# Gated linear attention and an MLP in one kernel: step 1 without halves, one transfer queue, a planner that may let an engine wait, attention visits placed anew

## The chip, the cores and the metric

The kernel runs on one core of one Trainium2 chip. Its engines are TensorE (PE in the rows; PEld is its loading of weights, which runs beside the products), VectorE (DVE), ScalarE (ACT), GpSimd (POOL) and SyncE (SP), which here only issues DMA transfers. The metric is the device time of one execution in microseconds (us); the median of several runs counts.

## The reference

Attention with a decaying state, and behind it a two-layer MLP on its output:

```python
f = 1 / (1 + exp(-f_logit))                  # q, k, v, f: (4 batches, 8 heads, 768 tokens, 48)
for t in range(768):
    state = f[:, :, t, :, None] * state + einsum('bhd,bhe->bhde', k[:, :, t], v[:, :, t])
    y[:, :, t] = einsum('bhd,bhde->bhe', q[:, :, t], state)
x = y.transpose(0, 2, 1, 3).reshape(3072, 384)
h = x @ w_in                                  # 384 -> 2048
g = where(h >= 1, h, where(h <= -1, 0, (h + 1)**2 / 4))
out = g @ w_out                               # 2048 -> 384
```

All is in float32.

## The kernel before

**Steps and units.** The 768 tokens are cut into six steps (0 to 5) of 128 tokens in each of the four batches, so that a step has 512 columns. A step's attention gives `x`, three tiles of 128 rows by 512 columns. The hidden layer is done in 16 pieces of 128 rows; one piece of one step is a *unit*, 96 in all, 0 to 95: units 0 to 15 belong to step 0, 16 to 31 to step 1, and so on. A unit has two halves on TensorE. The first half (`unit_1`, L250) puts nine products into one of two PSUM banks `ph`, the second half (`unit_2`, L274) puts nine products into the three banks `po`, which gather one step's output. Nine and not three, because each float32 operand is split into a high and a low part and three of the four combinations are summed: `w_hi` and `w_lo` for the weights, `ghi` and `glo` for the activation; `x` holds both parts. Between the halves stand five instructions: `act` (L253, ScalarE), `act` (L256, ScalarE), `act` (L261, VectorE), the rounding to `ghi` (L264, ScalarE) and the rest `glo` (L267, VectorE). The first half of unit u+1 lies between the two halves of unit u.

**Attention.** The eight heads are four pairs, and a step's attention runs two pairs at a time: gates (sigmoid L483, two scans L485 and L492, products with k and q L494 and L496), transposed keys `kn`, scores (L675), outputs (L762 from the states, L730 from the step's own values) and new states (L823; the first step uses L802 and others). The results leave PSUM as a rounded high part (ScalarE, L713) and a low part (VectorE, L714) into `x` and, for the fourth pair, into `y`. Those rows are then carried to where `x` wants them by six on-chip DMA transfers, the *moves* x<-y (L292); similar moves kq<-kq bring gated keys and queries into place. A first half of the next step's first unit needs all of its step's moves.

**Halves.** Step 1 alone (`HALVES = 1`) is handled in two halves of 256 columns: its gates, its attention and its moves come once for each two batches, and its first six units (`FIRST = 6`) are run in pairs on one half of the columns and then on the other, so that these units can start when only half of `x` is there. `order_of` holds that order.

**Weights.** They arrive packed in 25 pieces `raw`; ScalarE (L378, L383) and VectorE (L380, L384) unpack each into `w_hi` and `w_lo` during the first steps. Later the remaining transfers `raw` bring the packed weights once more, and VectorE reduces them (L394) for a test at the end: if some weight does not fit the packed form, a fallback computes everything again. `test` makes one number of it with a product of one column (L976) and a comparison; all engines load that number, `flag`, behind their last instruction (L1055) and branch on it (L1056).

**Who sets the order.** The code does not issue instructions where it stands. Each call of `add` gives a class `Plan` an operation with its engine, a cost and what it depends on; `order` then runs through time with those costs, and at each engine picks the operation that is most urgent (`late`, worked out from the end backwards) among those that could start. TensorE's operations keep the order of the code; for the others the planner's order is final, and each engine executes its own in that order. Where the plan shows a long gap on TensorE, `warm` fills it with products of zeros (L328). Where attention work stands among the units comes from two tables: `TURNS` (at which unit a pair's keys are transposed) and `VISITS` (at which units its scores, its states and its outputs come). A transfer is issued by `dma` (L287, SyncE) or `move` (L292), which takes SyncE and ScalarE in turn:

```python
def move(k, dst, src, *deps, near=NEAR):
    e, q = (("SP", nc.sync), ("ACT", nc.scalar))[k % 2]
```

An engine that issues a transfer waits at that point until what the transfer reads and overwrites is free, and whatever stands behind it on that engine waits with it.

## Time and profile before

| | before |
|---|---|
| runs | 480.68, 481.96, 482.08 us; median 481.96 us |
| span of the profiled execution | 480.9 us |
| TensorE busy | 470.6 us, 98% of the span |
| VectorE busy | 369.3 us, 77% |
| ScalarE busy | 264.7 us, 55% |
| GpSimd busy | 31.0 us, 6% |
| bytes read and written | 44.63 and 4.72 MB, 103 GB/s over the span |

The profile is of one execution. Times in it count from the start of the span. Matmuls are pipelined: the next starts before the one ahead is over, so the pace of TensorE is read from start to start and not from a row's duration. "PEld" rows are weight loads; a wait that ends there shows up on the products only if it outlasts the products ahead. In brackets a row tells how long its engine was idle before it and what released it. "SPq" and "ACTq" are the issues of transfers.

### The profile page before, as it was taken

To read this page: it belongs to the slowest core of one execution; us is meant where nothing else is said; L and a number is where in the kernel's file an instruction comes from. 1 tells how busy PE (TensorE), PEld (TensorE's weight loads), DVE (VectorE), ACT (ScalarE), POOL (GpSimd) and SP (SyncE) were. 2 spreads that over 40 slices of the span, in tenths; PEclk is the share of its full clock that TensorE was granted. 3 is DMA by queue.
4 is the path that set the end of the run, shared out by engine and by line. 5 is a ranking of instruction groups with operands and counts; after the bars stand their busy time and mean duration, and the time that the engine had idled before them with its cause. 6 is when DMAs were issued, how large, how long until landed. Compare 5 with 4: busy or idle time off the path is not lost.

```text
span 480.9 us, 11259 instructions
## 1 busy us (share of the span) xinstructions
PE 470.6 (98%) x4661; PEld 383.3 (80%) x4661; DVE 369.3 (77%) x715; ACT 264.7 (55%) x486; POOL 31.0 (6%) x76
## 2 busy tenths in 40 slices
PE   9989999999999999999999999999999999999994
PEld 4877888889988887887878878887888888888883
DVE  7979998859989999999997899675657545653332
ACT  4489998846355364555545464464545444544451
POOL 4201220100010101001000001000000000000000
PEclk9999999999999999999999999999999999999998
DMA  8689758055023061124144142143410242510001
GB/s 300 199 283 325 231 158 240 6 209 182 1 78 121 4 176 67 35 90 156 57 117 142 58 165 67 45 130 103 153 45 6 85 121 87 154 44 0 3 0 72
DMA packets 21866, 54.29 MB, mean 113 GB/s; under 512 B 3472, under 2 KB 6672, under 8 KB 21808
## 3 DMA queue, kind: packets, MB, share of 16 engines
q1 hardware_dynamic: 20464, 51.43, 33.1%
q10 hardware_dynamic: 1344, 2.07, 1.9%
q8 instruction: 38, 0.62, 0.6%
q14 instruction: 20, 0.16, 0.1%
HBM read 44.63 MB, written 4.72 MB: 103 GB/s over the span
## 4 chain that ended last, share of the span: by engine, by line
PE 73%; DVE 17%; DMA 5%; issue 2%; ACT 1%; SPq 0%; ACTq 0%; DVEq 0%
PE po L274 34%; PE ph L250 32%; DVE kn L708 6%; DMA raw<-in_w 2%; DVE glo L267 2%; PE pa L730 2%; PE pa L762 2%; DVE act L261 1%; DVE w L485 1%; DMA kq<-in_kq 1%; DVE kq L494 1%; PE ph L675 1%; DVE am L681 1%; DVE kq L496 1%; DMA f<-in_f 1%
## 5 line engine op out<-in xcount | busy, mean ns | idle before, releaser
L250 PE MATMUL ph<-x,w_hi 128*128 128x512 f32 (+1 forms) x606 | 146.8, 378 | 0.2
L250 PEld LDWEIGHTS ph<-x,w_hi 128*128 128x128 f32 x606 | 109.3, 188 | 22.5 <-DVE am L681 1.8
L253 ACT ACTIVATE act<-ph,half 128x512 f32<-128x512 f32 x96 | 65.8, 686 | 100.8 <-PE ph L250 91.6
L261 DVE SCALAR_TENSOR_TENSOR act<-ph,act 128x512 f32<-128x512 f32 x96 | 66.0, 687 | 62.2 <-ACT act L256 61.0
L264 ACT CAST ghi<-act 128x512 fp32r<-128x512 f32 x96 | 59.5, 620 | 85.5 <-DVE act L261 80.9
L274 PE MATMUL po<-ghi,w_hi 128*128 128x512 f32 (+1 forms) x306 | 87.6, 391 | 1.4 <-ACT ghi L264 1.3
L274 PE MATMUL po<-ghi,w_lo 128*128 128x512 f32 (+1 forms) x306 | 83.5, 378 | 0.0
L274 PE MATMUL po<-glo,w_hi 128*128 128x512 f32 (+1 forms) x306 | 83.4, 378 | 0.0
L267 DVE TENSOR_TENSOR glo<-act,ghi 128x512 fp32r<-128x512 f32 x96 | 66.0, 687 | 20.3 <-ACT ghi L264 18.2
L250 PE MATMUL ph<-x,w_lo 128*128 128x512 f32 (+1 forms) x303 | 81.2, 376 | 0.0
L708 DVE STREAM_TRANSPOSE kn<-kq 32x128 f32<-32x128 f32 x224 | 67.7, 302 | 3.5
L274 PEld LDWEIGHTS po<-glo,w_hi 128*128 128x128 f32 x306 | 55.3, 188 | 11.5 <-DVE glo L267 0.7
L274 PEld LDWEIGHTS po<-ghi,w_lo 128*128 128x128 f32 x306 | 55.4, 188 | 11.1
L274 PEld LDWEIGHTS po<-ghi,w_hi 128*128 128x128 f32 x306 | 52.6, 188 | 14.0 <-ACT ghi L264 4.3
L250 PEld LDWEIGHTS ph<-x,w_lo 128*128 128x128 f32 x303 | 55.3, 188 | 10.5
L256 ACT ACTIVATE act<-act 128x512 f32<-128x512 f32 x96 | 60.7, 632 | 3.0
L394 DVE TENSOR_REDUCE ok<-raw 128x1 f32<-128x512 f32 x48 | 31.5, 679 | 5.2 <-DMA raw<-in_w 5.2
L489 POOL COPY end<-w 128x4 f32<-128x4 f32 (+1 forms) x22 | 9.2, 416 | 263.8 <-DVE w L485 226.8
L485 DVE TENSOR_TENSOR_SCAN w<-f,least_w 128x512 f32<-128x512 f32 (+1 forms) x21 | 21.3, 1016 | 3.0 <-ACT f L483 2.2
L492 DVE TENSOR_TENSOR_SCAN f<-f,rec 128x512 f32<-128x512 f32 (+1 forms) x21 | 21.3, 1019 | 0.6
L378 ACT ACTIVATE bits<-raw,top_of 128x512 uint32<-128x512 fp8e4 (+1 forms) x25 | 18.2, 745 | 3.4 <-DMA raw<-in_w 3.4
L583 ACT ACTIVATE sd<-sd,kq 112x48 f32<-112x48 f32 x80 | 19.9, 327 | 0.0
(116 smaller groups left out, 387.5 us busy)
## 6 DMA issues: line engine op xcount, KB each, us to landing
raw<-in_w SPq DMA_DIRECT2D x24, 512.0 KB, 3.5
raw<-in_w SPq DMA_DIRECT2D x21, 511.6 KB, 4.7
kq<-in_kq SPq DMA_DIRECT2D x18, 512.0 KB, 5.1
out_y<-raw SPq DMA_DIRECT2D x18, 256.0 KB, 2.8
v<-in_v SPq DMA_DIRECT2D x10, 384.0 KB, 5.9
f<-in_f SPq DMA_DIRECT2D x13, 256.5 KB, 3.0
raw<-in_w SPq DMA_DIRECT2D x4, 382.9 KB, 6.6
f<-in_f SPq DMA_DIRECT2D x7, 128.5 KB, 4.4
```

Of the source, the lines that this page charges most:

```text
L250: nc.tensor.matmul(ps[:, to], w_in(w_hi if high else w_lo, j, kt), xt[:, kt, t, c], start=(n == 0), stop=(n == 8))
L253: nc.scalar.activation(a, ps, AF.Relu, bias=half, scale=0.5)
L256: nc.scalar.activation(a, a, AF.Square)
L261: nc.vector.scalar_tensor_tensor(out=a, in0=ps, scalar=1.0, in1=a, op0=ALU.max, op1=ALU.min)
L264: nc.scalar.copy(hi, a)
L267: nc.vector.tensor_tensor(out=lo, in0=a, in1=hi.bitcast(F32), op=ALU.subtract)
L274: nc.tensor.matmul(po[e][:, c], w_out(part, j, e), g[:, of], start=(j == 0 and n == 0 and c.start == 0), stop=(j == NJ - 1 and n == 2))
L394: seen.append(vec("dve", lambda z=z, op=op: nc.vector.tensor_reduce(out=ok[:, 1 + NG + z + c:2 + NG + z + c], in_=words_of(raw[2])[1].bitc ...
L485: s1 = vec(COST["scan"] if count == 1 else 602, lambda bwd=bwd, u0=u0, u1=u1: nc.vector.tensor_tensor_scan(out=wide(w[:, u0:u1]), data0=bw ...
L492: s2 = vec(COST["scan"] if count == 1 else 602, lambda fwd=fwd, b0=b0, b1=b1: nc.vector.tensor_tensor_scan(out=fwd, data0=fwd, data1=wide( ...
L583: nc.scalar.activation(ds[:, at + j * D:at + (j + 1) * D], state[:, q * B + b], AF.Copy, scale=pf[:R, j:j + 1])
L708: nc.vector.transpose(kn[n % 2][u:u + 32, ::-1, r:r + 32], src[:, :, u:u + 32])
```

## The change

**Step 1 without halves.** `HALVES`, `FIRST` and `order_of` go, with all that served them: gates, scores, outputs and moves of step 1 now come whole, as in the other steps, and its first six units use products of 512 columns. The inputs of step 1 are laid out like the others', and `f` loses one column.

**Moves.** All of them are issued by SyncE.

**Planner.** Before ScalarE or VectorE takes the most urgent operation that could start now, the planner looks whether a more urgent one becomes ready before that one would be over; if so, it leaves the engine idle until then. The rule is in `order`, with `PATIENCE = 0`. An operation can be given `late_by`, by which it counts as due sooner.

**Test.** The product of one column goes. The column `ok` is moved by a DMA into a row of `mask`, and two short instructions of VectorE (`decide`) make `flag` of it; `decide` counts as due 80 us sooner.

**Branch.** A call at the start, `mark_branch_hint_location("exact", "LikelyTaken")`, and a label at the branch of the fallback.

**Tables.** `TURNS` and `VISITS` have new numbers; where pairs come at other units, one row of each dictionary shows it in the diff.

```diff
+HOP, LANDING, PER_KB, NEAR, ADDING, PATIENCE, FLAG_BY = 200, 2000, 3.0, 3500, 1500, 0, 80000
...
-TURNS = {4: 5, 5: 6, 6: 11, 7: 11, 8: 20, 9: 20, 10: 25, 11: 25, 12: 29, ...
+TURNS = {4: 6, 5: 7, 6: 10, 7: 10, 8: 18, 9: 18, 10: 27, 11: 27, 12: 29, ...
-VISITS = {4: (6, 7, 9), 6: (11, 12, 13), ... 22: (70, 74, 75)}
+VISITS = {4: (7, 8, 9), 6: (10, 11, 12), ... 22: (75, 76, 77)}
...
-            o.late = min((u.late - (HOP if u.engine != o.engine else 0) for u in o.users), default=0) - tail
+            o.late = min((u.late - (HOP if u.engine != o.engine else 0) for u in o.users), default=0) - tail - o.late_by
...
+            if e in ("ACT", "DVE"):
+                first = a[0][2]
+                sooner = [r for r, _, o in q if o.late < first.late - PATIENCE and r < t + first.cost]
+                if sooner:
+                    free[e] = min(sooner)
+                    continue
             _, _, o = heappop(a)
...
-    def move(k, dst, src, *deps, near=NEAR):
-        e, q = (("SP", nc.sync), ("ACT", nc.scalar))[k % 2]
-        return add(e, "near", lambda: q.dma_start(dst, src), *deps, near=near)
+    def move(dst, src, *deps):
+        return add("SP", "near", lambda: nc.sync.dma_start(dst, src), *deps, near=NEAR)
...
+    tc.mark_branch_hint_location("exact", "LikelyTaken")
...
-    FIRST = 6
-    order_of = [[(u, None, ALL)] for u in range(NJ * HALVES)]
-    order_of += [[(NJ * HALVES + u + k, h, cols_of(k)) for k in range(2)] for h in range(2) for u in range(0, FIRST, 2)]
-    order_of += [[(u, None, ALL)] for u in range(NJ * HALVES + FIRST, NI * NJ)]
...
-        need = moved[i, h if h is not None or i != HALVES else 1] if i > 0 and (j == 0 or i == HALVES and j == FIRST) else []
+        need = moved[i] if i > 0 and j == 0 else []
...
+        def decide():
+            nc.vector.tensor_reduce(out=least_ok, in_=row_ok, axis=mybir.AxisListType.X, op=ALU.min)
+            nc.vector.tensor_scalar(out=flag, in0=least_ok, scalar1=0.5, scalar2=None, op0=ALU.is_lt)
...
-        o = add("PE", 500, lambda: nc.tensor.matmul(ps[0:1, 0:1], ok[:, 0:1], ones_col, start=True, stop=True), o, banks[0], set_consts)
-        vec("small", lambda: nc.vector.tensor_scalar(out=flag, in0=ps[0:1, 0:1], scalar1=127.5, scalar2=None, op0=ALU.is_lt), o)
+        o = move(row_ok, ok[:, 0:1], o)
+        vec("small", decide, o).late_by = FLAG_BY
...
-    with tc.If(bad > 0):
+    with tc.If(bad > 0, label="exact"):
```

**What moves in the order.** The rows below are each engine's own order in the program, without times. Line numbers and the numbers of tiles differ between the two programs: L250, L253, L256, L264, L274, L378, L383, L483, L583, L697 and L713 of before are L243, L246, L249, L257, L267, L369, L374, L451, L522, L627 and L643 of after, and ph_113, ph_114 and po_115 to po_117 are ph_112, ph_113 and po_114 to po_116.

TensorE at the start of step 1, before (unit 16's first half, and around it the second half of unit 15; x_86 is the step's `x`):

```order
L250 MATMUL ph_113<-x_86,w_hi 128x256 x6
L250 MATMUL ph_113<-x_86,w_lo 128x256 x3
L250 MATMUL ph_113<-x_86,w_hi 128x256 x6
L250 MATMUL ph_113<-x_86,w_lo 128x256 x3
L274 MATMUL po_115<-ghi_89,w_hi 128x512
L274 MATMUL po_115<-ghi_89,w_lo 128x512
L274 MATMUL po_115<-glo_91,w_hi 128x512
```

TensorE at the same place, after:

```order
L243 MATMUL ph_112<-x_86,w_hi 128x512 x6
L243 MATMUL ph_112<-x_86,w_lo 128x512 x3
L267 MATMUL po_114<-ghi_89,w_hi 128x512
L267 MATMUL po_114<-ghi_89,w_lo 128x512
L267 MATMUL po_114<-glo_91,w_hi 128x512
```

Where two units' products of 256 columns shared a bank, one unit's products of 512 columns stand.

ScalarE at the end of step 4, when the last outputs of its attention become `x` (x_85) and `y` (y_87), before (ghi_88 and ghi_89 are the roundings of two units in turn, sd the decayed states):

```order
L713 CAST x_85<-pa_110 112x512
L713 CAST y_87<-pa_111 112x512
L583 ACTIVATE sd<-sd,kq_68 112x48 x4
L264 CAST ghi_88<-act_83 128x512
L583 ACTIVATE sd<-sd,kq_69 112x48 x4
L292 DMA x_85<-y_87 16x1024 x3
L292 DMA kq_71<-kq_68 16x1028
L253 ACTIVATE act_84<-ph_114,half 128x512
L256 ACTIVATE act_84<-act_84 128x512
L292 DMA kq_71<-kq_69 16x1028
L292 DMA kq_71<-kq_70 16x1028
L264 CAST ghi_89<-act_84 128x512
```

ScalarE at the same place, after:

```order
L643 CAST x_85<-pa_109 112x512
L257 CAST ghi_89<-act_84 128x512
L643 CAST y_87<-pa_110 112x512
L522 ACTIVATE sd<-sd,kq_68 112x48 x4
L522 ACTIVATE sd<-sd,kq_69 112x48 x4
L451 ACTIVATE f_66<-f_66 128x513
L246 ACTIVATE act_83<-ph_112,half 128x512
L249 ACTIVATE act_83<-act_83 128x512
L257 CAST ghi_88<-act_83 128x512
L246 ACTIVATE act_84<-ph_113,half 128x512
L249 ACTIVATE act_84<-act_84 128x512
L257 CAST ghi_89<-act_84 128x512
```

The six issues are gone from ScalarE, and between `act` and `ghi` of a unit nothing stands any more.

ScalarE at the first unit, before (act_83 and ghi_88 are unit 0's, w_hi and bits those of weight pieces, kn transposed keys that the states need):

```order
L378 ACTIVATE bits_98<-raw_92,top_of 128x384
L713 CAST x_85<-pa_110 128x512
L483 ACTIVATE f_66<-f_66 128x257
L483 ACTIVATE f_67<-f_67 128x257
L383 CAST w_hi<-bits_98 128x3x128
L378 ACTIVATE bits_95<-raw_93,top_of 128x512
L253 ACTIVATE act_83<-ph_113,half 128x512
L256 ACTIVATE act_83<-act_83 128x512
L697 COPY kn_80<-pa_111 128x4x112
L697 COPY kn_81<-po_117 128x4x112
L383 CAST w_hi<-bits_95 128x512
L264 CAST ghi_88<-act_83 128x512
```

ScalarE at the same place, after:

```order
L643 CAST x_85<-pa_109 128x512
L451 ACTIVATE f_67<-f_67 128x513
L369 ACTIVATE bits_98<-raw_92,top_of 128x384
L246 ACTIVATE act_83<-ph_112,half 128x512
L249 ACTIVATE act_83<-act_83 128x512
L627 COPY kn_80<-pa_110 128x4x112
L627 COPY kn_81<-po_116 128x4x112
L374 CAST w_hi<-bits_97 128x512
L257 CAST ghi_88<-act_83 128x512
L374 CAST w_hi<-bits_98 128x3x128
L246 ACTIVATE act_84<-ph_113,half 128x512
L369 ACTIVATE bits_95<-raw_93,top_of 128x512
```

The piece in bits_95 stands behind unit 0's `ghi` instead of ahead of its first `act`; the whole loads of `f` (513 columns) replace halves of 257.

Elsewhere: the order of TensorE in the changed program has two products of zeros between the `w_hi` and the `w_lo` products of unit 4's first half; there were none. On VectorE `decide` stands after unit 77's `glo` and ahead of unit 78's `act`, 18 units before the end. On SyncE the move of `ok` stands right ahead of the six moves of step 5, and the load of `flag` right behind them, ahead of the transfers of step 4's output; before, `flag` was loaded behind those. No engine's order has a hint instruction ahead of the branch at L938; those of the two loops in the fallback are there in both programs.

## Rows read from the trace of the kernel before

**Rows 1.** the page, busy time of each engine

```profile
PE 470.6 (98%) x4661; PEld 383.3 (80%) x4661; DVE 369.3 (77%) x715; ACT 264.7 (55%) x486; POOL 31.0 (6%) x76
```

**Rows 2.** timeline of TensorE in a later unit: start, duration, work

```profile
430.98 1.52 PE L250 MATMUL ph<-x,w_hi 128*128 128x512 f32 x6
...
433.02 0.84 PE L274 MATMUL po<-ghi,w_hi 128*128 128x512 f32 x3
```

**Rows 3.** groups of TensorE by shape: count, busy, mean ns, idle before

```profile
L250 PE MATMUL ph<-x,w_hi 128*128 128x256 f32 x72 | 10.6, 283 | 0.0
...
L250 PE MATMUL ph<-x,w_lo 128*128 128x256 f32 x36 | 6.3, 283 | 0.0
```

**Rows 4.** timeline of TensorE in step 1, halves

```profile
112.96 0.88 PE L250 MATMUL ph<-x,w_hi 128*128 128x256 f32 x6
...
114.04 0.88 PE L250 MATMUL ph<-x,w_hi 128*128 128x256 f32 x6
```

**Rows 5.** timeline of TensorE at the end of step 4

```profile
325.83 0.84 PE L250 MATMUL ph<-x,w_lo 128*128 128x512 f32 x3
327.51 0.73 PE L274 MATMUL po<-ghi,w_hi 128*128 128x512 f32 x2 [0.84 <-ACT ghi L264]
```

**Rows 6.** timeline of ScalarE at the end of step 4

```profile
323.93 0.63 ACT L256 ACTIVATE act<-act 128x512 f32<-128x512 f32 x1
325.59 1.21 ACTq L292 DMA_DIRECT2D kq<-kq  x2
326.84 0.62 ACT L264 CAST ghi<-act 128x512 fp32r<-128x512 f32 x1 [2.28 <-DMA kq<-kq]
```

**Rows 7.** timeline of TensorE ahead of a later group of scores

```profile
246.48 0.27 PE L675 MATMUL ph<-kq 48*64 48x64 f32 x1 [0.17 <-DVE act L261]
```

**Rows 8.** timeline of the weight loads just behind

```profile
249.99 0.76 PEld L250 LDWEIGHTS ph<-x,w_hi 128*128 128x128 f32 x4 [0.52 <-DVE am L681]
```

**Rows 9.** timeline of ScalarE at the first unit

```profile
27.81 0.76 ACT L378 ACTIVATE bits<-raw,top_of 128x512 uint32<-128x512 fp8e4 x1 [0.36 <-DMA raw<-in_w]
...
31.07 0.63 ACT L264 CAST ghi<-act 128x512 fp32r<-128x512 f32 x1
```

**Rows 10.** groups of TensorE from 26 to 33 us

```profile
L802 PE MATMUL pa<-sd,kn 128*48 128x48 f32 x32 | 1.0, 212 | 1.0 <-ACT kn L697 1.0
L274 PE MATMUL po<-ghi,w_hi 128*128 128x512 f32 x3 | 1.0, 429 | 0.5 <-ACT ghi L264 0.5
```

**Rows 11.** waits: waiting line, releaser, total us, times, longest

```profile
PEld po L274 <- ACT ghi L264: 4.3, 8, 1.3
```

**Rows 12.** timeline of SyncE at the end of step 5

```profile
390.50 1.78 SPq L292 DMA_DIRECT2D x<-y  x3
```

**Rows 13.** timeline of TensorE, last attention products of step 5

```profile
387.44 0.63 PE L730 MATMUL pa<-am,v 64*48 64x64 f32 x32
```

**Rows 14.** transfers issued from 386 to 400 us: KB, us to landing

```profile
x<-y SPq DMA_DIRECT2D x3, 64.0 KB, 2.4
```

**Rows 15.** timeline of TensorE, last attention products of step 2

```profile
169.70 0.63 PE L730 MATMUL pa<-am,v 64*48 64x64 f32 x32
```

**Rows 16.** timeline of SyncE at the end of step 2

```profile
174.99 1.77 SPq L292 DMA_DIRECT2D x<-y  x3
```

**Rows 17.** transfers issued from 170 to 183 us

```profile
x<-y SPq DMA_DIRECT2D x3, 64.0 KB, 3.9
```

**Rows 18.** the chain of waits at unit 32: start, us, work

```profile
182.13 2.34 PE ph L250 x9
```

**Rows 19.** busy us (instructions) of each engine in a window, clock, DMA

```profile
40.00:60.00 20.00, 20.00 (x178) 15.97 (x177) 19.37 (x37) 18.38 (x38) 3.90 (x6) 1.00 0.82 274
```

**Rows 20.** waits of SyncE's queue at the branch

```profile
SPq L1056 <- SPq L1056: 3.5, 1, 3.5
```

**Rows 21.** timeline of SyncE, last issues

```profile
473.74 1.69 SPq L287 DMA_DIRECT2D out_y<-raw  x3
```

**Rows 22.** the page, transfers of the output

```profile
out_y<-raw SPq DMA_DIRECT2D x18, 256.0 KB, 2.8
```

More of the change, by code (lines that the diff above doesn't have):

```diff
@@ L272, in mm_out @@
                 part, g = ((w_hi, hi), (w_lo, hi), (w_hi, lo))[n]
-                nc.tensor.matmul(po[e][:, c], w_out(part, j, e), g[:, of], start=(j == 0 and n == 0 and c.start == 0), stop=(j == NJ - 1 and n == 2))
+                nc.tensor.matmul(po[e], w_out(part, j, e), g, start=(j == 0 and n == 0), stop=(j == NJ - 1 and n == 2))
     def copy_out(e, o):
@@ L556, in elementwise @@
         else:
-            c["lv"] = dma(v[k], vv[i, p // 2], 384, before, att[2]["st"], moved[HALVES, 1])
-        if NP - 1 in mine:
-            every = range(NT * i, NT * i + NT)
-            cols = slice(HW * h, HW * h + HW) if by_half else slice(0, 2 * N + B) if i else slice(0, N)
-            gone = [old(NP * i - j, "sc", "y", "tr", "db") for j in ((1, 2, 3, 4) if i == HALVES + 1 else (1,))]
-            for t, m in enumerate(every):
-                o = gates_of[m]
-                d = [o[a][h] for a in ("km", "qm", "pf")] if by_half else [o["km"], o["qm"], o["pf"][0]] if i else o["km"]
-                to = [move(k, kq[NP - 1][z + 16 * t:z + 16 * t + 16, cols], kq[t][r:r + 16, cols], d, set_kq, gone, near=NEAR) for k, (r, z) in enumerate(((48, 0), (112, 64)))]
-                o["to"] = o.get("to", []) + to
-                c.setdefault("to", []).extend(to)
@@ L587, in blocks @@
-    def blocks(n):
-        i, p = pairs[n]
-        if i == HALVES:
-            return [(2 * (p % 2) + e, 2 * (p // 2) + m) for e in range(2) for m in range(2)]
-        return [(p, m) for m in range(B)]
+            c["lv"] = dma(v[k], vv[i, p // 2], 384, old(n - 4, "y", "st"), att[2]["st"], moved[1] if i > 1 else None)
+        if p == NP - 1:
+            cols = slice(0, 2 * N + B) if i else slice(0, N)
+            gone = old(n - NP, "sc", "y", "tr", "db")
+            c["to"] = []
+            for t, m in enumerate(ours):
+                o = gates_of[m]
+                d = [o["km"], o["qm"], o["pf"][0]] if i else o["km"]
+                o["to"] = [move(kq[NP - 1][z + 16 * t:z + 16 * t + 16, cols], kq[t][r:r + 16, cols], d, set_kq, gone) for r, z in ((48, 0), (112, 64))]
+                c["to"] += o["to"]
@@ new lines, in elementwise, with decayed @@
+        c["kq"] = c["to"] if p == NP - 1 else [gates_of[m][a] for m in ours for a in ("km", "qm")]
+        c["db"] = []
+        if i > 0:
+            at = n % 2 * B * D
+            pf = whole(kq[p])
+            d = c["to"] if p == NP - 1 else gates_of[NT * i + p]["pf"][0]
+            def decayed():
+                for b in range(B):
+                    nc.scalar.activation(ds[:, at + b * D:at + (b + 1) * D], state[:, p * B + b], AF.Copy, scale=pf[:R, b:b + 1])
+            c["db"].append(sca(B * COST["decay"], decayed, d, state_of[i - 1, p // 2], old(n - 2, "y", "se"), set_ds))
@@ L605, in emit @@
                 opened["bank"] = None
-            for m, (q, b) in enumerate(blocks(n)):
+            for m in range(B):
                 for (a, z), (_, ps, _) in zip(HEADS, held):
-                    nc.tensor.matmul(ps[:, m], key(n, q, b)[a:z], query(n, q, b)[a:z], start=True, stop=True)
+                    nc.tensor.matmul(ps[:, m], key(n, m)[a:z], query(n, m)[a:z], start=True, stop=True)
         c["sc"] = add("PE", "scores", emit, c["kq"], [d for h in held for d in h[2]])
@@ L671, in emit @@
             for e in range(2):
-                for m, (q, b) in enumerate(blocks(n + e)):
+                p = (n + e) % NP
+                for m in range(B):
                     for k, h in TILES:
                         (a, z), half = HEADS[h], slice(T * k, T * k + T)
-                        nc.tensor.matmul(by_block(held[h][1])[half, e * B + m], key(n + e, q, b)[a:z, half],
-                                         query(n + e, q, b)[a:z, T * (1 - k):][:, :T], start=True, stop=True)
+                        nc.tensor.matmul(by_block(held[h][1])[half, e * B + m], key(p, m)[a:z, half],
+                                         query(p, m)[a:z, T * (1 - k):][:, :T], start=True, stop=True)
         c["sc"] = d["sc"] = add("PE", "both", emit, c["kq"], d["kq"], [h[2] for h in held])
@@ L818, in emit @@
             for e in range(2):
-                for m, (q, t) in enumerate(blocks(n + e)):
+                for m in range(B):
                     a = (e * B + m) * D
@@ L1014, in gla_moe @@
             groups.setdefault(u, []).append((kind, n))
-    for u in range(len(order_of)):
+    for u in range(NI * NJ):
         unit_1(u)
@@ L1038, in gla_moe @@
     test()
-    for u in range(len(order_of) - 3, len(order_of)):
+    for u in range(NI * NJ - 3, NI * NJ):
         unit_2(u)
```

271 lines of the change are left out of this document (78 added, 193 removed).

## The prediction

> **What bounds the kernel now.** I read the page's totals first: TensorE is busy 470.6 of 480.9 us [rows 1]. A kernel like that can get faster in three ways only: less work on TensorE, fewer waits inside its stream, or a shorter tail after its last product. So the next views were TensorE's groups by shape (what work could go), the order of time around every place where TensorE stood still (whom it waited for), and the end of the span.
>
> The work: a first or second half of a unit is nine products of 512 columns, and from one such half to the next 2.04 us pass (430.98 to 433.02), so 0.227 us for one product [rows 2]. Step 1 has, for its first six units, products of 256 columns instead: 72 in one group and four groups of 36, 216 in all [rows 3]. Nine of them take 1.08 us (112.96 to 114.04), 0.120 us each [rows 4], which is more than half of 0.227: two halves cost more than one whole.
>
> The waits: the worst one lies at the end of step 4. The last product of a first half starts at 325.83 + 2 x 0.227 = 326.28 and would hand over at 326.51; the next product starts at 327.51, and the row names ScalarE's `ghi` as what it waited for [rows 5]. ScalarE shows why: after the square at 323.93 its queue holds two DMA issues, for transfers kq to kq, that could start only at 325.59; the cast to `ghi` stands behind them, at 326.84 [rows 6]. Two smaller stops follow a step earlier, while ScalarE issues the moves of that step: 0.17 us before the scores at 246.48 [rows 7], 0.52 us of weight loading before 249.99 [rows 8]. At the first unit the same engine is late for another reason: `act` of unit 0 is queued behind a weight piece whose transfer landed only at 27.81, so that `ghi` starts at 31.07 [rows 9], and TensorE stood 1.0 us before the states and 0.5 us before the second half of unit 0 [rows 10]. Over the whole run the weight loads of second halves waited 4.3 us for `ghi`, in 8 places, the longest 1.3 [rows 11].
>
> **The change, part by part**, against the span of 480.9 us; the median of the runs, 481.96, lies 1.1 above that, and I carry the difference over.
>
> *Step 1 without halves.* 216 products of 256 columns become 108 of 512: 216 x 0.120 = 25.9 us go, 108 x 0.227 = 24.5 us come. TensorE never rests in that stretch, so all of it shows: **-1.4 us**. What the halves had bought was time: the first six units of step 1 could start with half of the tokens. Now unit 16 needs all six moves of x. The new tables put the last outputs of step 1 at unit 12, so 7 halves of a unit, 7 x 2.04 = 14.3 us, lie between them and unit 16; the longest way of x that I work out below for six moves is 11.6 us. I cost this at nothing; the cover is those 14.3 us.
>
> *All on-chip transfers on SyncE.* 39 DMA issues leave ScalarE, about 0.6 us each (two in 1.21 us [rows 6]), and with them every stop of ScalarE's queue for their semaphores. At the end of step 4 `ghi` then follows the square directly: the whole stop goes, **-1.0 us**. Of the two stops at 246 to 250, 0.17 + 0.52 us, VectorE was named as the releaser and it was late behind ScalarE: I take half, **-0.3 us**. The rest of the 4.3 us, some 2.5 us in six places after the 1.3 at step 4 and the 0.5 at unit 0, holds the ordinary hand-over as well; no row says which of it stood behind an issue, so between 0 and 2.5, and I take **-0.5 us**. The issues are not gone, they stand on SyncE: three took 1.78 us there [rows 12], so six take 3.6, and the sixth starts 3.0 us after the first. Queued behind them are loads of weights for the test, of `f`, of `kq` and of `v`, and TensorE waits for the moves themselves. I cost it at nothing because of this margin: in step 5 the last attention product starts at 387.44 and takes 0.63 [rows 13], and the first issue came at 390.50, 2.4 us after its end; with six in a row and 2.4 us to landing [rows 14] the last piece would be there 2.4 + 3.0 + 2.4 = 7.8 us after that product. There the new tables leave TensorE 5 halves, 10.2 us, before it needs the piece. In step 2, with a busier VectorE, the first issue came 4.7 us after the product (170.33 [rows 15] to 174.99 [rows 16]), landing took 3.9 us [rows 17]: 11.6 us, while unit 32 began 11.8 us after the product (182.13 [rows 18]), after 5 halves and a group of scores, and the new tables leave the same there and at step 4. That is just enough, and the third product of a unit, the one that needs the last two pieces, starts 0.45 us later still.
>
> *The planner idles engines for urgent work; attention placed anew.* At the first unit the new ScalarE order has `act` of unit 0 ahead of the weight piece instead of behind it. That can give back up to the 1.5 us of [rows 10]. But from 40 to 60 us VectorE was busy 19.4 and ScalarE 18.4 of 20 us [rows 19]: what TensorE gains there it may lose at the next weight piece. Bounds 0 and 1.5; I take the middle, **-0.8 us**. Against it: SyncE now issues two whole loads of `f` ahead of the fourth weight piece and only after all six early moves, and the two filler products inside unit 4 show that the planner itself sees a gap in TensorE there. They cost 2 x 0.227 = 0.45 us if nothing waits there; I book **+0.5 us**, between 0 and 1.5 (a weight piece as late as the wait of 1.0 us at the first unit, on top of the fillers). In the later steps visits move by at most 5 units, with whole halves of a unit between producer and consumer: nothing.
>
> *The test by DMA.* One product of one column leaves TensorE. Two waits come. On SyncE the move of `ok` stands ahead of the six moves of step 5 and waits for VectorE's comparison; that comparison stands ahead of the subtractions that the moves need anyway, so it holds up none. On VectorE `decide` waits for that move to land, 2.4 to 3.9 us by [rows 14, 17]; queued behind it are `act` and `glo` of unit 78, and TensorE's second half of 78 waits for those. Between comparison and `decide` stand four instructions, two of them subtractions for which the last attention product must be over, so the move has most likely landed. Between 0 and about 2 us (3.9 less one half of a unit, 2.04, of room); I take nothing. `flag` is now loaded by SyncE ahead of step 4's output transfers; they are free until the end: nothing.
>
> *The branch announced early.* After its last issue SyncE reached the branch and needed 3.5 us to go on [rows 20], which is the cost that an announcement could lower. But the order of the changed program holds no hint instruction ahead of that branch on any engine. So I expect no change at the end.
>
> Sum: -1.4 - 1.0 - 0.3 - 0.5 - 0.8 + 0.5 = **-3.5 us**: span 477.4, median 481.96 - 3.5 = **478.5 us**.
>
> On the moves the rows show 0.59 us per issue on SyncE (1.78 / 3 [rows 12]) against 2.4 to 3.9 us until landing [rows 14, 17], so a second queue saved about 3 x 0.59 = 1.8 us per set of six. The Trainium skill (DMA: Bandwidth & Descriptors, "Rules for kernel authors") says that spreading DMAs over engines gains no bandwidth, since all run on the same 16 DMA engines, and saves only the time of issuing. It speaks against the change by just that time: where there is no margin a set would cost its 1.8 us, where there is one, nothing; the rows give a margin, so the sum stays.
>
> **The rivals.** (1) *The early stretch gives it back.* With VectorE and ScalarE as full as [rows 19] shows, TensorE runs into weight pieces: the -0.8 and the -0.5 are gone and the +0.5 becomes +1.5. Then -1.4 - 1.0 - 0.3 + 1.5 = -1.2: 480.8 us. For it: both engines are nearly full, and the planner expects a gap. Against it: both have less to do there than before (no issues, no half-size instructions).
>
> (2) *Slower: x arrives late at the step ends.* The place is the first half of units 32, 64 and 80, with the least room. Price: each microsecond by which the way of x exceeds the room goes straight onto TensorE. It decides when the first issue comes more than 4.8 us after the product in step 5 (10.2 - 3.0 - 2.4) and more than 4.9 in steps 2 and 4 (11.8 - 3.0 - 3.9). To end 0.3% slower it must cost 3.5 + 1.4 = 4.9 us, 1.6 us at each of the three: 483.4 us. For it: step 2 had 4.7. Against it: step 5 had 2.4, ScalarE rounds sooner without issues in its queue, and the planner may now hold VectorE free for the urgent subtractions.
>
> (3) *The end gets shorter after all*, because the branch target comes sooner (a hint that takes effect, or another position of the target in memory). The last issue was over at 475.43 (473.74 + 1.69 [rows 21]), and outputs land 2.8 us after issue [rows 22]; SyncE went on 3.5 us after its branch [rows 20]. So 0.7 to 1.1 us at most were not covered by the transfer; about 1.0 off the sum: 477.5 us. The Trainium skill (Runtime: NRT & Kernel Launch, "Instruction fetch mechanics") says that a taken branch whose target is not in the loaded window must wait for a fetch by DMA; the 3.5 us agree with such a wait, and by that rule an announcement that is really in the program would pay.
>
> (4) *ScalarE was the brake nearly everywhere*: all of the 1.5 and all of the 2.5 us go, and both stops at 246 to 250: -1.4 - 1.0 - 0.7 - 2.5 - 1.5 + 0.5 = -6.6: 475.4 us.
>
> **How the numbers follow.** Chances: forecast 0.50, rival 1 0.22, rival 2 0.10, rival 3 0.10, rival 4 0.08. The forecast's own spread is about 1.5 us either way by the bounds of its terms. The range goes from 476.0, which leaves out most of rival 4, to 481.6, which takes in rival 1 with the 0.8 us of a `decide` that waits a little. About 0.3% (1.4 us) is what a measurement of this kernel can tell from no change. Faster than 480.5: the forecast but for 0.02, rivals 3 and 4, and two fifths of rival 1: 0.75. Within 0.3%: the rest of rival 1, the 0.02, and 0.01 of rival 2 with a single late step: 0.16. Slower: 0.09.
>
> **What would show it.** In the profile after: no 256-column product; no DMA issue on ScalarE; the gap of TensorE at the end of step 4 gone, with `ghi` right behind the square; the sum of weight loads waiting for `ghi` well under 4.3 us; the idle time before the states under 1.0. Wrong would be: a wait of TensorE for the transfers of x at units 32, 64 or 80; TensorE waiting for weight pieces between 30 and 60 us; VectorE idle before `decide` with TensorE idle behind it; SyncE going on much sooner than 3.5 us after its branch.

## The result and the profile after

The changed kernel takes 476.61 us (median of 4 runs, 475.88 to 478.38) against 481.98 us before: ratio 0.9886, interval 0.9845 to 0.9928, 5.4 us. Some executions of a kernel run slower than the rest at a lower granted clock; ratios leave these out, medians have them in. Run once more (e1) it gave the same ratio, 0.9886 (0.9861 to 0.9910). The forecast was 478.5. The profiled execution after is the longest of its four: span 476.5, 4.4 us under [rows 1]'s 480.9.

The page, busy time of each engine (answers [rows 1]), and TensorE's groups by shape (answer [rows 3]; the 256-column groups are gone, two products of zeros have come):

```profile
PE 467.5 (98%) x4553; PEld 378.5 (79%) x4553; DVE 371.0 (78%) x699; ACT 266.0 (56%) x481; POOL 25.8 (5%) x66
```

```profile
L243 PE MATMUL ph<-x,w_hi 128*128 128x512 f32 x570 | 145.1, 390 | 0.0
...
L319 PE MATMUL po<-zeros 128*128 128x512 bf16 x2 | 0.6, 384 | 0.0
```

Where the time went is read from the start of a unit's first half in both traces (the row of its six `w_hi` products; before, after, difference):

| | before | after | after - before |
|---|---|---|---|
| unit 2 | 33.92 | 32.42 | -1.50 |
| unit 4 | 44.00 | 44.20 | +0.20 |
| unit 16 (step 1) | 104.43 | 105.19 | +0.76 |
| unit 22 (halves over) | 131.52 | 130.99 | -0.53 |
| unit 32 (step 2) | 182.14 | 180.61 | -1.52 |
| unit 49 | 262.38 | 258.80 | -3.59 |
| unit 64 (step 4) | 333.76 | 329.16 | -4.61 |
| unit 80 (step 5) | 406.50 | 402.28 | -4.22 |
| end of the last product | 474.34 | 469.97 | -4.37 |

So the early stretch lost, the halves gave 1.3, units 22 to 64 gave 4.1, step 4 took 0.4 back. At the end of step 4 TensorE no longer stops (answers [rows 5]): from the start of the last three products of a first half to the next group 0.68 us pass, three times 0.227. On ScalarE `ghi` follows the square with only VectorE's `act` between (answers [rows 6]). TensorE, then ScalarE:

```profile
321.04 0.84 PE L243 MATMUL ph<-x,w_lo 128*128 128x512 f32 x3
321.72 0.84 PE L267 MATMUL po<-ghi,w_hi 128*128 128x512 f32 x3
```

```profile
322.64 0.63 ACT L249 ACTIVATE act<-act 128x512 f32<-128x512 f32 x1
324.04 0.62 ACT L257 CAST ghi<-act 128x512 fp32r<-128x512 f32 x1 [0.76 <-DVE act L254]
```

In the list of waits (line, releaser: total us, times, longest) the 4.3 us of [rows 11] are 0.3. A wait for `glo` is new:

```profile
PEld po L267 <- ACT ghi L257: 0.3, 1, 0.3
...
PE po L267 <- DVE glo L260: 1.4, 1, 1.4
```

It lies at unit 3. TensorE's order of time there (and the two products of zeros at 45.60), then ScalarE's:

```profile
41.12 0.86 PE L267 MATMUL po<-ghi,w_lo 128*128 128x512 f32 x3
43.41 0.96 PE L267 MATMUL po<-glo,w_hi 128*128 128x512 f32 x3 [1.43 <-DVE glo L260]
...
45.60 0.60 PE L319 MATMUL po<-zeros 128*128 128x512 bf16 x2
```

```profile
41.27 0.75 ACT L369 ACTIVATE bits<-raw,top_of 128x512 uint32<-128x512 fp8e4 x1 [1.15 <-DMA raw<-in_w]
```

VectorE's unpacking of that weight piece stood ahead of `glo`. What unit 2 had gained by [rows 9, 10] was lost to the next piece, as rival 1 has it. Over 40 to 60 us VectorE and ScalarE were busy less than in [rows 19], TensorE too:

```profile
40.00:60.00 20.00, 18.57 (x104) 14.64 (x100) 17.29 (x27) 16.33 (x31) 1.90 (x3) 1.00 0.65 224
```

The moves of step 5 (answer [rows 12 to 14]): SyncE's six issues and the move of `ok`, then the transfers' landing times, then VectorE's `decide`, which did not wait, then the start of unit 80:

```profile
390.60 0.54 SPq L283 DMA_DIRECT2D mask<-ok  x1
394.64 3.72 SPq L283 DMA_DIRECT2D x<-y  x6
```

```profile
x<-y SPq DMA_DIRECT2D x1, 64.0 KB, 2.3
mask<-ok SPq DMA_DIRECT2D x1, 0.5 KB, 1.9
```

```profile
394.53 0.26 DVE L854 TENSOR_REDUCE ok<-mask 1x1 f32<-1x128 f32 x1
```

```profile
402.28 1.07 PE L243 MATMUL ph<-x,w_hi 128*128 128x512 f32 x4
```

The sixth issue began about 3.1 us after 394.64 and landed at 400.0, 2.2 us ahead of unit 80. SyncE's wait at the branch is what it was in [rows 20]:

```profile
SPq L938 <- SPq L938: 3.5, 1, 3.5
```

### The profile page after: what moved, and what is told of

Its sections match the earlier page's. It is cut to its first block, busy times and chain, and to the rows that moved or that the text cites. A ratio compares the mean times of both kernels' runs of the same rounds, so it can differ in the third digit from the quotient of the medians.

```text
span 476.5 us, 10934 instructions
## 1 busy us (share of the span) xinstructions
PE 467.5 (98%) x4553; PEld 378.5 (79%) x4553; DVE 371.0 (78%) x699; ACT 266.0 (56%) x481; POOL 25.8 (5%) x66
## 4 chain that ended last, share of the span: by engine, by line
PE 94%; DMA 2%; ACT 1%; DVE 1%; issue 0%; SPq 0%; ACTq 0%
PE po L267 41%; PE ph L243 39%; DMA raw<-in_w 2%; PE ph L319 2%; PE pa L657 2%; PE pa L679 2%; PE ph L605 2%; PE pa L727 1%; PE ph L727 1%; PE ph L557 1%; PE pa L605 0%; ACT bits L369 0%; PE po L538 0%; PE pa L752 0%; PE pa L624 0%
## 5 line engine op out<-in xcount | busy, mean ns | idle before, releaser
L243 PE MATMUL ph<-x,w_hi 128*128 128x512 f32 x570 | 145.1, 390 | 0.0
L246 ACT ACTIVATE act<-ph,half 128x512 f32<-128x512 f32 x96 | 66.0, 687 | 112.7 <-PE ph L243 112.1
L243 PEld LDWEIGHTS ph<-x,w_hi 128*128 128x128 f32 x570 | 106.8, 188 | 22.7 <-ACT w_hi L374 0.3
L257 ACT CAST ghi<-act 128x512 fp32r<-128x512 f32 x96 | 59.6, 621 | 64.1 <-DVE act L254 63.6
L267 PE MATMUL po<-ghi,w_hi 128*128 128x512 f32 x288 | 86.8, 403 | 0.0
L267 PE MATMUL po<-glo,w_hi 128*128 128x512 f32 x288 | 83.2, 390 | 1.4 <-DVE glo L260 1.4
L267 PE MATMUL po<-ghi,w_lo 128*128 128x512 f32 x288 | 83.3, 390 | 0.0
L243 PE MATMUL ph<-x,w_lo 128*128 128x512 f32 x285 | 80.2, 390 | 0.0
L267 PEld LDWEIGHTS po<-glo,w_hi 128*128 128x128 f32 x288 | 53.9, 188 | 13.8 <-DVE glo L260 2.2
L267 PEld LDWEIGHTS po<-ghi,w_lo 128*128 128x128 f32 x288 | 54.1, 188 | 11.7
L243 PEld LDWEIGHTS ph<-x,w_lo 128*128 128x128 f32 x285 | 53.5, 188 | 11.2
L249 ACT ACTIVATE act<-act 128x512 f32<-128x512 f32 x96 | 60.7, 632 | 3.0
L267 PEld LDWEIGHTS po<-ghi,w_hi 128*128 128x128 f32 x288 | 51.5, 188 | 11.1 <-ACT ghi L257 0.3
L457 POOL COPY end<-w 128x4 f32<-128x4 f32 (+1 forms) x19 | 7.4, 391 | 320.0 <-DVE w L453 288.3
L369 ACT ACTIVATE bits<-raw,top_of 128x512 uint32<-128x512 fp8e4 (+1 forms) x25 | 18.2, 745 | 5.3 <-DMA raw<-in_w 5.2
L522 ACT ACTIVATE sd<-sd,kq 112x48 f32<-112x48 f32 x80 | 19.6, 326 | 0.0
```

The costliest lines, as they stand in the source:

```text
L243: nc.tensor.matmul(ps, w_in(w_hi if high else w_lo, j, kt), xt[:, kt, t], start=(n == 0), stop=(n == 8))
L246: nc.scalar.activation(a, ps, AF.Relu, bias=half, scale=0.5)
L249: nc.scalar.activation(a, a, AF.Square)
L257: nc.scalar.copy(hi, a)
L267: nc.tensor.matmul(po[e], w_out(part, j, e), g, start=(j == 0 and n == 0), stop=(j == NJ - 1 and n == 2))
L522: nc.scalar.activation(ds[:, at + b * D:at + (b + 1) * D], state[:, p * B + b], AF.Copy, scale=pf[:R, b:b + 1])
```

## The experiments

Every kernel was timed in five rounds against the kernel before. From e2 on no products of zeros stand inside units, so that the planner's guesses of gaps don't cost time themselves. The kernel before took 482.7 us beside e1 to e4, 481.9 beside e5 to e8, 482.2 beside e9 to e11 and 482.3 beside e12; across these groups the ratios compare better than the medians.

| kernel | us, median | ratio to before, interval |
|---|---|---|
| e1 changed kernel again | 477.05 | 0.9886 (0.9861 to 0.9910) |
| e2 without the two fillers | 476.06 | 0.9881 (0.9853 to 0.9910) |
| e3 e2, two queues | 479.19 | 0.9935 (0.9913 to 0.9957) |
| e4 e2, no idling | 482.70 | 1.0003 (0.9988 to 1.0018) |
| e5 halves removed alone | 484.55 | 1.0056 (1.0028 to 1.0085) |
| e6 e5 with one queue | 481.74 | 0.9992 (0.9973 to 1.0011) |
| e7 e5 with idling | 486.89 | 1.0100 (1.0067 to 1.0134) |
| e8 e2, old tables | 488.52 | 1.0093 (1.0061 to 1.0126) |
| e9 e2, hint emitted | 474.86 | 0.9861 (0.9835 to 0.9887) |
| e10 e2, old test | 476.19 | 0.9878 (0.9854 to 0.9903) |
| e11 e2, no due time | 478.71 | 0.9939 (0.9920 to 0.9958) |
| e12 e9, joint visit | 475.12 | 0.9851 (0.9828 to 0.9874) |

**e1, the changed kernel again.** No edit.

> The changed kernel once more, nothing left out. In its first profile unit 2 started 1.5 us earlier than before, but unit 4 0.2 us later: VectorE's glo of unit 3 stood behind a weight piece that landed at 41.27 us, and TensorE waited 1.4 us. That execution (478.4) was the longest of four (475.9 to 478.4). If this wait is an accident of when the piece lands, it is shorter or gone in some executions: the median is 476.6 within 0.7, and single runs spread over 2 us, while before they spread over less than 1.5. If it is fixed by the order, the second profile shows it again within 0.3 us and the spread has another cause.

Median 477.05. Its profile shows no stop at unit 3: unit 4 starts at 42.53, not 44.20, and unit 16 at 103.57, 0.86 us ahead of before. The wait of 1.43 us was an accident of that execution. The execution took 478.3 us all the same, since its end was longer: 8.2 us from the last product to the end of the span, 6.6 in the first profile, with SyncE's last three issues spread over 3.24 us instead of 1.69.

**e2, no fillers.**

```diff
-                elif gap > 500:
-                    warm(int(gap * 0.9 / 230))
```

> The changed kernel without the two products of zeros in unit 4; all else the same. They took 0.45 us where nothing waited, so 476.2, 0.4 under the changed kernel, if TensorE does not wait there. If a weight piece is what TensorE waits for at that point, the time does not change (within 0.3 us of the changed kernel).

1.0 us under e1 by the medians, 0.05% by the ratios, with intervals of 0.3% either way: not told apart. In the traces from unit 4 to unit 5 4.29 us pass in e2 and 4.54 in e1. So the fillers cost 0.25 us, where I had worked out 0.45.

**e3, two queues.**

```diff
-    def move(dst, src, *deps):
-        return add("SP", "near", lambda: nc.sync.dma_start(dst, src), *deps, near=NEAR)
+    def move(dst, src, *deps):
+        e, q = (("SP", nc.sync), ("ACT", nc.scalar))[turn_of["k"] % 2]
+        turn_of["k"] += 1
+        return add(e, "near", lambda: q.dma_start(dst, src), *deps, near=NEAR)
```

> The kernel of e2 with the transfers x<-y and kq<-kq taken by SyncE and ScalarE in turn, as before; planner, tables and test stay. Theory A, that the stops of TensorE between units 22 and 64 (4.1 us in the two profiles) came from ScalarE's queue being held at its DMA issues: most of them come back, 478.5 to 480. Theory B, that they went because the planner lets an engine wait for urgent work: they stay away, within 0.7 us of e2. Theory C, that the new tables took them away: within 0.7 us of e2 as well.

3.1 us over e2 by the medians, 2.6 by the ratios: the time is the one of theory A, but the trace bears out its cause only for a small part. ScalarE at the end of step 5 shows one place; a square waits behind an issue, and TensorE lost 0.43 us between units 78 and 80:

```profile
396.84 1.99 ACTq L287 DMA_DIRECT2D x<-y  x3
398.88 0.63 ACT L249 ACTIVATE act<-act 128x512 f32<-128x512 f32 x1 [1.43 <-DMA x<-y]
```

The others lie between units 32 and 40, 2.1 us, and are not behind issues. At the longest, 1.10 us at 215.81, TensorE waits for VectorE's masked scores `am`; those come behind eight transposes and two subtractions on VectorE, while ScalarE issues nothing there:

```profile
211.32 2.52 DVE L642 STREAM_TRANSPOSE kn<-kq 32x128 f32<-32x128 f32 x8
213.87 1.29 DVE L648 TENSOR_TENSOR x<-pa,x 112x512 fp32r<-112x512 f32 x2
215.08 0.68 DVE L615 TENSOR_TENSOR am<-pa,mask_t 128x512 f32<-128x512 f32 x1
```

In e2 the second eight transposes do not stand there. With two queues the planner also arrives at another order on VectorE, and that costs more here than the issues.

**e4, no idling.**

```diff
-            if e in ("ACT", "DVE"):
+            if e in ():
```

> The kernel of e2 with a planner that never leaves an engine idle for a more urgent operation, as before; transfers all on SyncE, tables and test new. Theory A: within 0.7 us of e2. Theory B: the stops come back, 478.5 to 480. Theory C: within 0.7 us of e2. In the early stretch the first unit's act may stand behind a weight piece again, which costs up to 1.5 us at unit 2 and may save as much at unit 4.

6.6 us over e2 by the medians, 5.9 by the ratios, as slow as the kernel before: theory B holds, and its size was underestimated. The two traces agree within 0.4 us at unit 16; from there to unit 64 e4 loses 6.1. One of its stops, in the order ScalarE, VectorE, TensorE: the square is over at 229.57, but VectorE's `act` comes only behind eight transposes (two operations of the plan, four each), 1.9 us later:

```profile
228.94 0.63 ACT L249 ACTIVATE act<-act 128x512 f32<-128x512 f32 x1
```

```profile
228.88 2.53 DVE L638 STREAM_TRANSPOSE kn<-kq 32x128 f32<-32x128 f32 x8
231.43 0.69 DVE L254 SCALAR_TENSOR_TENSOR act<-ph,act 128x512 f32<-128x512 f32 x1
```

```profile
232.83 0.96 PE L267 MATMUL po<-ghi,w_hi 128*128 128x512 f32 x3 [0.75 <-ACT ghi L257]
```

Not every stop is VectorE's alone. At the end of step 0 TensorE waits 0.69 us at 105.99. There ScalarE's `act` stood behind a sigmoid whose `f` landed only at 102.32; the transposes added 0.4 us to that:

```profile
102.32 0.64 ACT L451 ACTIVATE f<-f 128x513 f32<-128x513 f32 x1 [1.66 <-DMA f<-in_f]
```

The same pattern stood in the trace of before, ahead of the stop of [rows 7] and ahead of one at 222.31, where I had not looked at VectorE:

```profile
243.18 2.52 DVE L708 STREAM_TRANSPOSE kn<-kq 32x128 f32<-32x128 f32 x8
245.73 0.69 DVE L261 SCALAR_TENSOR_TENSOR act<-ph,act 128x512 f32<-128x512 f32 x1
```

```profile
219.80 1.23 DVE L492 TENSOR_TENSOR_SCAN f<-f,rec 128x512 f32<-128x512 f32 x1
220.94 0.67 DVE L261 SCALAR_TENSOR_TENSOR act<-ph,act 128x512 f32<-128x512 f32 x1
```

**e5 to e7, step 1 without halves, alone and with one further part.** e5 is the changed kernel with the `move` of e3 (two queues), the edit of e4, the old `TURNS` and `VISITS`, the old test of e10 and no fillers; e6 takes the new `move` back in, e7 the idling.

> Step 1 without halves and nothing else of the change: transfers by two engines in turn, no idling, old tables, old test, no announcement; no products of zeros inside units. The 216 products of 256 columns take 25.9 us, the 108 that replace them 24.5. Expected 1.4 us under the kernel before, 481.3, if TensorE is as full as before. Rival: the halves had let TensorE start step 1 early; if x now comes late at unit 16, TensorE waits there and the time is that of before or more.

2.7 us slower than before, with single runs from 482 to 490 us; the profiled one, 482.5, is among the fastest. In it the halves' 1.3 us do not show, since new stops take them: TensorE lost 1.3 us ahead of 102.67 and, between units 16 and 22, 0.45 and 0.54 at 107.83 and 120.33. At the first of these ScalarE was held at its three issues of step 1's moves and began `act` 2.9 us after its last work. VectorE's twelve transposes, which stand ahead of the next `act`, added 0.24 us. ScalarE, VectorE, TensorE:

```profile
96.78 2.78 ACTq L288 DMA_DIRECT2D x<-y  x3
99.60 0.69 ACT L247 ACTIVATE act<-ph,half 128x512 f32<-128x512 f32 x1 [2.86 <-PE po L268]
100.32 0.63 ACT L250 ACTIVATE act<-act 128x512 f32<-128x512 f32 x1
```

```profile
97.38 3.79 DVE L644 STREAM_TRANSPOSE kn<-kq 32x128 f32<-32x128 f32 x12
101.19 0.69 DVE L255 SCALAR_TENSOR_TENSOR act<-ph,act 128x512 f32<-128x512 f32 x1
```

```profile
102.67 0.98 PE L268 MATMUL po<-ghi,w_hi 128*128 128x512 f32 x3 [1.15 <-ACT ghi L258]
```

A further 1.3 us were lost inside the scores at unit 70, with nothing to wait for (below). What the longest runs lost is not in any trace.

> The kernel of e5 with all transfers x<-y and kq<-kq issued by SyncE. Theory A, ScalarE's held queue was the cause of the stops between units 22 and 64: 3 to 4 us under e5. Theory B, after the profile without idling: most stops came from VectorE, where a scan of 1.2 us or a row of transposes of up to 2.5 us had begun when the act of a unit became ready; then only the stop of 1.0 us at the end of step 4 goes, 1.1 us under e5, within 0.7.

2.8 us under e5, between the two theories, and the traces bear out neither. The stop of 1.0 us at the end of step 4 is in neither of them (e5 lost 0.13 us at its place), and over units 22 to 64 they differ by 0.2 us. Of the 2.3 us by which e6 is ahead at its last product, 1.8 had come by unit 22. Against before the gain only balances what e5 lost.

> The kernel of e5 with the planner that may idle an engine for urgent work; two queues, old tables and test. Theory A: within 0.7 us of e5, since ScalarE's queue is held as before. Theory B: the stops behind scans and transposes go, 2 to 3 us under e5; those at ScalarE's issues stay. Its planner saw gaps in TensorE with the old tables, which speaks for new stops in other places; then it is at or above e5.

2.3 us over e5. Up to unit 94 its trace is 4.1 us ahead of e5's (theory B), 3.1 of it gained by unit 22, but then TensorE waits for the test: a planner that idles had put the reductions of the weights off to the last units, and the one-column product stood in TensorE's stream behind them.

```profile
463.42 0.84 PE L244 MATMUL ph<-x,w_lo 128*128 128x512 f32 x3
469.58 0.19 PE L865 MATMUL pa<-ones_col,ok 128*1 128x1 f32 x2 [5.32 <-DVE ok L857]
469.70 1.65 PE L268 MATMUL po<-ghi,w_hi 128*128 128x512 f32 x3
```

Behind it the granted clock was 0.50, in this window (seventh figure: clock):

```profile
469.60:475.00 5.40, 5.40 (x15) 4.22 (x16) 0.15 (x1) 0.00 (x0) 0.00 (x0) 0.50 0.01 3
```

**e8, old tables.** The `TURNS` and `VISITS` of before in e2.

> The kernel of e2 (all of the change, without the two products of zeros) with the old tables of where attention stands. If the placement is a matter of fractions of a microsecond, as costed: within 0.7 us of e2, or 0.4 us faster, since the old table joins two visits at unit 70. If planner and tables only work together, because idling for urgent work pushes the rest back until it is late itself: slower than e2 by 1.5 us or more, with stops of TensorE at the transposed keys, the scores or the moves of x.

12.5 us over e2 by the medians, 10.2 by the ratios, the largest effect of all. Its single runs spread from 482 to 491 us, and the profiled one is the longest, so its stops explain that execution; what the others lost is in no trace. The longest stop: VectorE idles 4.59 us ahead of a reduction for the test, whose transfer SyncE issued only just ahead of the six moves of step 4; `glo` stands behind that reduction, and TensorE waits 3.20 us for it. VectorE, SyncE, TensorE:

```profile
326.40 1.28 DVE L385 TENSOR_REDUCE ok<-raw 128x1 f32<-128x512 f32 x2 [4.59 <-DMA raw<-in_w]
```

```profile
318.86 1.35 SPq L280 DMA_DIRECT2D raw<-in_w  x1
320.25 3.68 SPq L283 DMA_DIRECT2D x<-y  x6
```

```profile
328.34 0.97 PE L267 MATMUL po<-glo,w_hi 128*128 128x512 f32 x3 [3.20 <-DVE glo L260]
```

A second stop, 2.00 us ahead of the outputs at 386.62, came from VectorE's `am`. So with idling and due time in place, the tables are not a matter of fractions: at the stop shown an urgent reduction waits for a transfer that the plan had earlier. e7, with the old tables and idling but two queues and the old test, has no such stop there; the old tables without the due time alone were not run.

**e9, the hint emitted.**

```diff
-    tc.mark_branch_hint_location("exact", "LikelyTaken")
+    tc.mark_branch_hint_location("exact", "LikelyTaken", engines=nc.engines)
```

> The kernel of e2 with the announcement of the branch given for every engine by name, so that a hint instruction really stands at the start of each engine's program; the change's own form leaves none. In e2 SyncE went on 3.0 us after its branch, at about 472.3, while the outputs issued last had landed by about 472. If the hint takes the wait for the branch target away, the end is set by the outputs: 0.3 to 1.0 us under e2, and the row of SyncE waiting for itself at the branch falls under 1 us. If a hint given 470 us ahead does nothing, the time is that of e2 within 0.5 us and the row stays near 3.

1.2 us under e2 by the medians, 1.0 by the ratios (the intervals overlap), the fastest kernel so far. SyncE's wait for itself at the branch in e2, then in e9:

```profile
SPq L936 <- SPq L936: 3.0, 1, 3.0
```

```profile
SPq L936 <- SPq L936: 2.4, 3, 1.4
```

The one wait became three short ones, and those are for the outputs: by the records of the trace SyncE went on 0.5 us after the branch (469.02 to 469.54), where it took 3.0 in e2, and then waited for outputs until 471.5. From the last product to the end of the span 5.4 us pass, 6.0 in e2. But e3, which has no hint in its program, shows the same: SyncE went on 0.5 us after its branch, and its wait is split too.

```profile
SPq L940 <- SPq L940: 2.8, 4, 1.3
```

Without a hint the time from the branch to the next record of SyncE lies between 0.5 (e3) and 4.1 us (e4), with it at 0.5 in both traces (e9, e12). So the hint agrees with a short wait, but that it is the hint, and not where the target lies in memory, isn't shown.

**e10, old test; e11, no due time.**

```diff
-        o = move(row_ok, ok[:, 0:1], o)
-        vec("small", decide, o).late_by = FLAG_BY
+        ps = wide(pa[0])
+        o = add("PE", 500, lambda: nc.tensor.matmul(ps[0:1, 0:1], ok[:, 0:1], ones_col, start=True, stop=True), o, banks[0], set_consts)
+        vec("small", lambda: nc.vector.tensor_scalar(out=flag, in0=ps[0:1, 0:1], scalar1=127.5, scalar2=None, op0=ALU.is_lt), o)
```

> The kernel of e2 with the old test: a product of one column on TensorE between units 93 and 95, no move by DMA, no earlier due time. As costed (nothing, since the product is short): within 0.5 us of e2. By what e7 showed, a planner that idles puts the reductions of the weights off until the last units, the product stands in TensorE's stream and waits about 5 us for them, and the clock granted afterwards is the lower one for some us: 481 to 484.

0.1 us over e2: no difference. With the new tables the reductions were done at 461.5, ahead of the product, so the wait of e7 does not come.

```diff
-        vec("small", decide, o).late_by = FLAG_BY
+        vec("small", decide, o)
```

> The kernel of e2 with the test by DMA, but without the due time 80 us ahead. The reductions then stand in the last units again and flag comes after VectorE's last copies, so no product waits; the load of flag on all engines waits for comparison, move (2.4 us to landing) and two short instructions. Expected 2 to 4 us over e2, all of it behind the last product, if the due time is what the test needs; within 0.5 us of e2 if the reductions are early anyway.

2.6 us over e2, as expected, all behind the last product: `decide` comes after the last copies and waits for the move, and `flag` is loaded after that.

```profile
470.08 0.28 DVE L854 TENSOR_REDUCE ok<-mask 1x1 f32<-1x128 f32 x1 [1.72 <-DMA mask<-ok]
```

**e12, a joint visit.**

```diff
-20: (63, 68, 74), 22: (75, 76, 77)}
+20: (63, 68, 74), 22: (74, 76, 77)}
```

> The kernel of e9 with one number of the new table changed: the scores of step 5's second two pairs come at unit 74, right behind step 4's... that is, behind the outputs of the two pairs ahead of them, instead of at unit 75. In the kernel before such a visit was joined at unit 70, and there TensorE changed from small to large products one time less, 0.24 us. In e5 to e8, with the old table, TensorE stood 1.0 to 1.7 us in the middle of the scores of that joint visit, with no semaphore to wait for. If 160 small products in a row are what runs TensorE dry, the same stop shows here: 0.8 to 1.5 us over e9. If the stop belongs to something else of the old table, the change is only the saved 0.24 us: 474.6, which one can't tell from e9.

What tells it from e9 is its trace alone: 0.38 us less between units 74 and 76, and no stop. The medians, 475.12 and 474.86, don't tell them apart. In e5 the scores of the joint visit show the stop, in e12 not (last figures: idle before, and its releaser):

```profile
L611 PE MATMUL pa<-kq 48*64 48x64 f32 x32 | 1.4, 219 | 1.3 <-issue 1.3
```

```profile
L605 PE MATMUL pa<-kq 48*64 48x64 f32 x32 | 1.1, 218 | 0.0
```

So 160 small products in a row don't make it by themselves.

## Why the prediction was right, and where not

The time lies in the range and the sign was right; the gain was forecast at 3.5 us and is 5.4. By steps:

- *Halves, -1.4.* From unit 16 to 22 the trace shows -1.29: the arithmetic of 0.120 against 0.227 holds. That the rest of it costs nothing held only in company: alone (e5) the same edit lost 2.7 us. The cover that I named, 14.3 us for the moves, was there (the six issues of step 1 start at 96.22, unit 16 at 105.19); what I missed is that, with two queues and no idling, ScalarE's issues of those moves and VectorE's scans and transposes then stand ahead of urgent work (102.67, 107.83 and 120.33 in e5).
- *One queue, -1.0 - 0.3 - 0.5 = -1.8.* Undone in e3 it costs 3.1, added in e6 it gives 2.8: the sign is right, the size too small by about 1. The mechanism, ScalarE held at its issues, is shown at single places: 0.4 us in e3, most of 1.3 in e5, and the stop of 1.0 us at the end of step 4 in the trace of before. That stop went as told, but it is gone in the traces of e3 and e5 too, where ScalarE still issues; so one queue alone is not what took it away. Most of what e3 loses (2.1 of 2.6 us) comes from the order on VectorE, so that the sum of this term came near is in part luck. The margins held: no wait for x at units 32, 64 or 80. The Trainium skill's rule on spreading DMAs (DMA: Bandwidth & Descriptors, "Rules for kernel authors") agrees in that two queues brought no earlier landing: 2.4 and 3.9 us after the issue on two [rows 14, 17], 2.3 on one in step 5.
- *Idling: -0.8 at the first unit, "in the later steps ... nothing".* This is the step that failed, with the reading of [rows 7, 8] and of the remaining 2.5 us of [rows 11] behind it. I wrote that VectorE "was late behind ScalarE". In the trace of before it was late behind its own scans and transposes: at 246.48 and 222.31 ScalarE's square had been over for 1.8 and 1.3 us when `act` began. Units 22 to 64 gave 4.1 us where I had 1.8. With the other parts in place (e1, e2, e10, e11 and e12 pass these units in 198.2 us each), idling gives 3.5 us there (e2 against e4) and one queue 2.1 (e2 against e3). These don't add up to a share for each, since e5, with neither, passes the same units 1.5 us faster than before. A stop also costs more than its wait: behind the one at 222.31 three products took 0.82 us to the next group, 0.68 elsewhere.

```profile
222.31 0.98 PE L274 MATMUL po<-ghi,w_hi 128*128 128x512 f32 x3
223.13 0.63 PE L274 MATMUL po<-ghi,w_lo 128*128 128x512 f32 x2
```

- *Tables, nothing.* Directly they cost 0.4 us (the visit of unit 70 split in two, units 64 to 80). But idling is worth 6.6 us with them, and with the old ones in their place the whole change is slower than before. A price for each alone did not exist; that a sum of such prices came within 2 us of the measured gain is in part luck.
- *Early stretch, -0.8 + 0.5.* -0.86 at unit 16 in e1 and +0.76 in the first profile: the weight piece decides, and of rival 1 the early part came true in the first profile.
- *Test, nothing; end, nothing.* Right (e10, and 3.5 us at the branch). Rival 3's price was about right: with a hint that is really emitted 1.0 to 1.2 us go by the runs, 0.65 of them behind the last product in the traces. The rule of the Trainium skill (Runtime: NRT & Kernel Launch, "Instruction fetch mechanics"), that a taken branch can have to wait for its target, agrees with 3.0 us in e2 and 0.5 in e9. It leaves open why e3 took 0.5 without a hint.
- Rival 4 named a time, 475.4, nearer to the 476.6 than the forecast, but its cause, ScalarE at nearly every stop, is not what the trace of before shows. Rival 2 did not come.

## What to carry to other kernels

When TensorE waits, read two engines back before naming the cause: the engine that released it may itself have been held by instructions of its own that stand ahead of the urgent one, or by one that waits for a transfer. Here a scheduler that may leave an engine idle for an urgent operation took such stops away (5.9 to 6.6 us). Its rule, due times and tables of places depend on each other, so each should be tried with the others in place, and alone only to learn. One edit to the order moves instructions on every engine: whether a cause was right is read from the places of the stops, not from the time. After an edit that announces a branch, look into the program for the hint: here it was missing.

## What the runs showed that was not expected

- After three stops of TensorE its granted clock fell to the lower level (0.50, 1.2 GHz) for some us: the one of 5.32 us in e7 (0.427 us per product behind it instead of 0.227) and those of 3.20 and 2.00 us in e8. In e8 the clock was 0.57 behind the stop of 3.20 and 0.50 behind that of 2.00:

```profile
329.00:333.00 4.00, 4.00 (x12) 3.12 (x11) 2.50 (x5) 0.55 (x2) 0.00 (x0) 0.57 0.34 119
388.60:394.00 5.40, 5.40 (x17) 4.18 (x14) 2.34 (x4) 0.00 (x0) 0.00 (x0) 0.50 0.33 97
```

  The stop in e7 cost 8.0 us in all (unit 94 to the last product, against e5). The stops of 1 us in before and after left the clock at 1.00.
- In e5 to e8 TensorE stood 1.0 to 1.7 us in the midst of the scores of unit 70 with no semaphore to wait for; the kernel before has the same visit without the stop, e12 a like one without it. The cause stays open.
